# Moving and resizing the convolution chunks of four batches in a fused conv and low-rank mixer kernel

## The chip, the cores and the metric

One NeuronCore of one Trainium2 chip runs the whole kernel. The metric is the device time of one execution in microseconds (us); each version was run several times and medians are quoted.

## The reference, cut to what matters

`x` is (8, 4224, 192) in float32. A causal depthwise convolution of seven taps with softmaxed weights, eight heads of 24 channels, gives `y`; then a low-rank mixer over the sequence and a channel MLP:

```python
out = np.einsum('hk,bskhg->bshg', w, x_unf)      # the conv: y
...
h = xt @ U @ V                                    # sequence mixing, rank 32
u = x + h.transpose(0, 2, 1)                      # here x is y
ch = np.maximum(u @ w_ch1, 0.0) @ w_ch2           # 192 -> 768 -> 192
return (u + ch).astype(np.float32)
```

## The kernel before: the parts that matter

Every batch has 33 tiles of 128 positions; eight tiles make one of 33 groups. The program is scheduled by hand. From batch 3 on it runs in stages: W1 of three groups (the wide matrix product, its relus on ScalarE and VectorE), then W2 of three groups in twelve pieces, with other work put between the pieces. A dictionary says what comes ahead of which piece: `c4:0:3:AAD` is the conv of batch 4, from head 0, three heads, whose results are copied out of PSUM, the memory that matmuls write (evacuated), in turn by ScalarE (A), ScalarE and VectorE (D); `t` is the projection by U, `s` its sum, `h` the product with V, `x5:3` starts the shift copies of batch 5.

```python
        elif k < 10:
            b = k - 2
            at = {
                1: [f"c{b}:0:3:AAD"],
                2: [f"c{b}:3:3:AAD"],
                3: [f"c{b}:6:2:A"] + ([f"x{b + 1}:3"] if b + 1 < B else []),
                5: [f"t{b}", hs[0]],
                7: [f"s{b}"],
                8: [hs[1]],
                11: [hs[2]],
            }
```

The conv of a head is eight matmuls into two PSUM banks (there are eight, taken in rotation). Half of them read `xb`, a copy of x in which half of the partitions are shifted by a block:

```python
    def conv32(b, h0, nh, engs):
        ...
        for n in range(nh):
            ...
            pp = [bank(), bank()]
            for cg in range(4):
                t, w, st = (
                    (xt[b], bands[h // HQ][:, h % HQ, QB : 2 * QB], 1 + cg // 2)
                    if cg % 2
                    else (xbt[b], band2[:, h, :], cg // 2)
                )
                for r in range(2):
                    ...
                    nc.tensor.matmul(out=pp[r][...], lhsT=w[hr], rhs=t[hr, ...], ...)
            for part in range(2):
                evac(engs[(2 * n + part) % len(engs)], yt[b][...], pp[part][...])
```

GpSimd builds `xb` in six steps of a copy each (the second has a small copy more). There is one buffer for it, so the first copy for the next batch waits for the last conv matmul of this one. With `x5:3` three copies are issued right then; the others are issued one by one during the next W1, each behind a transfer of the x after that, and the transfers are held until W1 has come so far:

```python
        return [
            same(0, m),
            same(m, NB0, (NB0, NB1)),
            ahead(0, 0, m),
            ahead(0, m, NB0),
            ahead(1, 0, m),
            ahead(1, m, NB1),
        ]
...
        for g in gs1:
            ends = w1(g, RELU0 if g == 1 else RELU)
            for b, blocks in LOADS.items():
                for q, (gb, m) in enumerate(blocks):
                    if gb == g:
                        x_load(b, q, ends[m])
                        if steps:
                            steps.pop(0)()
```

Of the kernel before, what the change touches and what calls it, by code (L numbers as in the profile page):

```python
# [14 lines left out]
def kernel(  # L15
# [12 lines left out]
    B, S, D = x.shape  # L28
# [611 lines left out]
    for k in range(5, 14):  # L640
        gs = list(range(3 * k - 9, 3 * k - 6))
        hs = [f"h{g}" for g in range(nh, min(nh + 3, NG))] + [None] * 3
        nh = min(nh + 3, NG)
        if k == 5:
            at = {
                2: ["c3:0:3:AAD"],
                3: ["c3:3:3:AAD"],
                4: ["c3:6:2:A", "x4:3"],
                5: [hs[0]],
                6: ["t3"],  # L650
                8: ["s3", hs[1]],
                11: [hs[2]],
            }
        elif k < 10:
            b = k - 2
            at = {
                1: [f"c{b}:0:3:AAD"],
                2: [f"c{b}:3:3:AAD"],
                3: [f"c{b}:6:2:A"] + ([f"x{b + 1}:3"] if b + 1 < B else []),
                5: [f"t{b}", hs[0]],  # L660
                7: [f"s{b}"],
                8: [hs[1]],
                11: [hs[2]],
            }
        else:
            at = {0: [hs[0]], 4: [hs[1]], 8: [hs[2]]}
        SLOTS.append((gs, gs, {p: [w for w in what if w] for p, what in at.items()}))
# [180 lines left out]
```

## Time and profile before

| | kernel before |
|---|---|
| median of three runs | 325.3 us (325.18 to 325.31) |
| span of the profiled run | 323.5 us |
| TensorE busy | 317.1 us, 98% |
| ScalarE, VectorE, GpSimd busy | 170.4, 269.1, 142.7 us |
| stages of batches 3 to 7 | 28.30, 28.05, 28.28, 28.13, 28.12 us |

A stage is measured in the timeline, from the first matmul of its W1 to that of the next. In the chain of waits each line is start, duration and what the chain went through; in the timeline each line is start, duration, engine, source line, operation, tiles, shapes and count. L554 is W1, L583 W2, L339 the conv, L402 the projection, L305 the later shift copies, L568 ScalarE's relu. The lines themselves are in the prediction below.

### The profile page before, as it was taken

The numbers are of one execution on the slowest core, as the hardware profiler recorded it, in microseconds if no ns is written. First come the engines' busy times: TensorE is split into PE (matmuls) and PEld (weight loads), VectorE is DVE, ScalarE is ACT, GpSimd is POOL, SyncE is SP. The second block draws the span as 40 slices with busy tenths as digits, with TensorE's granted clock in tenths as the row PEclk, the third lists the DMA queues.
The fourth block names the chain that finished last, engine by engine and source line by source line (L and its number), as shares of the span: only waits on it lengthen the run. The fifth ranks groups of instructions, "written<-read, shape, count | busy, mean of one in ns | idle before, by whom it ended". The sixth has DMA issues, their size and how long they took to land.

```text
span 323.5 us, 9584 instructions
## 1 busy us (share of the span) xinstructions
PE 317.1 (98%) x3996; PEld 223.2 (69%) x3996; DVE 269.1 (83%) x551; ACT 170.4 (53%) x344; POOL 142.7 (44%) x111
## 2 busy tenths in 40 slices
PE   6999999999999999999999999999999999999996
PEld 3757676478677647866864784587797497487495
DVE  6769989987977986998798699879898897896864
ACT  1766624860874397088339708824903902912920
POOL 8664179729947694786859497000000000000000
PEclk9999999999999999999999999999999999999999
DMA  8999993999996899699699976139269059048035
GB/s 104 192 192 178 209 211 99 203 195 248 210 153 180 229 175 169 170 162 195 166 238 183 192 162 181 33 112 244 58 168 267 8 149 268 25 121 271 2 119 176
DMA packets 122907, 53.52 MB, mean 165 GB/s; under 512 B 87760, under 2 KB 122832, under 8 KB 122864
## 3 DMA queue, kind: packets, MB, share of 16 engines
q1 hardware_dynamic: 84528, 38.08, 47.0%
q0 software_dynamic: 38192, 14.73, 39.6%
q8 instruction: 31, 0.51, 0.7%
q14 instruction: 12, 0.10, 0.1%
q10 hardware_dynamic: 144, 0.10, 0.1%
HBM read 29.49 MB, written 25.95 MB: 171 GB/s over the span
## 4 chain that ended last, share of the span: by engine, by line
PE 92%; ACT 3%; DMA 2%; DVE 1%; issue 0%; POOL 0%; POOLq 0%
PE ps L583 42%; PE ps L554 39%; PE ps L339 3%; PE ps L457 3%; DMA x_sb<-in_x_dram 2%; PE ps L402 2%; ACT rl_sb L568 2%; PE ps L369 1%; ACT y_sb L256 1%; PE ps L509 1%; DVE u_sb L479 1%; DVE rl_sb L570 1%; PE ps L524 0%; PE ps L428 0%; POOL x_sb L79 0%
## 5 line engine op out<-in xcount | busy, mean ns | idle before, releaser
L568 ACT ACTIVATE rl_sb<-ps 128x512 bf16<-128x512 f32 x233 | 124.3, 603 | 108.0 <-PE ps L554 96.0
L583 PE MATMUL ps<-W_sb,rl_sb 128*128 128x192 bf16 x1584 | 141.9, 246 | 0.2
L583 PEld LDWEIGHTS <-rl_sb 128*128 128x128 bf16 x1584 | 128.1, 98 | 13.5 <-issue 13.1
L554 PE MATMUL ps<-uT,W_sb 64*128 64x512 bf16 x1188 | 131.7, 376 | 0.0
L570 DVE TENSOR_SCALAR rl_sb<-ps 128x512 bf16<-128x512 f32 x163 | 105.3, 688 | 15.7 <-PE ps L554 15.4
L554 PEld LDWEIGHTS <-W_sb 64*128 64x128 bf16 x1188 | 66.9, 94 | 60.5 <-issue 3.9
L592 DVE TENSOR_TENSOR out_sb<-ps,u_sb 128x384 f32<-128x384 f32 (+1 forms) x133 | 70.4, 550 | 25.9 <-PE ps L583 25.4
L305 POOL COPY xb_sb<-x_sb 32x3072 bf16<-32x3072 bf16 (+1 forms) x24 | 67.6, 2826 | 0.7
L479 DVE TENSOR_TENSOR u_sb<-y_sb,ps 128x192 bf16<-128x192 bf16 (+1 forms) x168 | 66.3, 461 | 0.0
L293 POOL COPY xb_sb<-x_sb 128x3072 bf16<-128x3072 bf16 x12 | 32.6, 2744 | 34.6 <-PE ps L339 25.7
L256 ACT ACTIVATE y_sb<-ps 128x384 bf16<-128x384 f32 (+4 forms) x90 | 38.2, 514 | 10.7 <-PE ps L339 7.9
L79 POOL DMA_DIRECT2D x_sb<-in_x_dram x32 | 27.1, 849 | 17.5 <-PE ps L554 10.5
L258 DVE CAST y_sb<-ps 128x408 bf16<-128x408 f32 (+4 forms) x36 | 19.2, 578 | 1.1 <-PE ps L369 0.9
L457 PE MATMUL ps<-tt_sb,V_sb 32*128 32x192 bf16 x264 | 12.4, 246 | 0.1
L339 PE MATMUL ps<-xb_sb,band 64*32 64x384 bf16 x192 | 12.1, 332 | 0.0
L339 PE MATMUL ps<-x_sb,band 64*32 64x384 bf16 x192 | 12.1, 333 | 0.0
L457 PEld LDWEIGHTS <-V_sb 32*128 32x128 bf16 x264 | 4.7, 92 | 7.3 <-issue 7.3
L416 ACT ACTIVATE tt_hi<-ps 128x192 bf16<-128x192 f32 x8 | 2.6, 331 | 10.9 <-PE ps L402 10.9
L369 PE MATMUL ps<-x_sb,band 64*64 64x240 bf16 (+3 forms) x192 | 8.1, 276 | 0.3 <-DMA x_sb<-in_x_dram 0.3
L369 PEld LDWEIGHTS <-band 64*64 64x64 bf16 x192 | 6.0, 106 | 2.2 <-issue 1.5
L339 PEld LDWEIGHTS <-band 64*32 64x32 bf16 x384 | 4.5, 89 | 4.1 <-issue 3.0
L402 PE MATMUL ps<-y_sb,U_sb 128*32 128x192 bf16 x258 | 7.4, 247 | 0.0
(65 smaller groups left out, 69.0 us busy)
## 6 DMA issues: line engine op xcount, KB each, us to landing
out_dram<-out_sb SPq DMA_DIRECT2D x131, 192.0 KB, 2.7
x_sb<-in_x_dram POOLq DMA_DIRECT2D x14, 384.0 KB, 7.3
x_sb<-in_x_dram POOLq DMA_DIRECT2D x7, 432.0 KB, 7.3
x_sb<-in_x_dram POOLq DMA_DIRECT2D x7, 408.0 KB, 8.0
x_sb<-in_x_dram POOLq DMA_DIRECT2D x1, 504.0 KB, 7.6
uT<-u_sb SPq DMA_TRANSPOSE x31, 3.9
x_sb<-in_x_dram POOLq DMA_DIRECT2D x1, 480.0 KB, 5.9
W_sb<-in_moe_w_ch_dram POOLq DMA_DIRECT2D x2, 192.0 KB, 7.6
```

Of the source, the lines that this page charges most:

```text
L79: return nc.gpsimd.dma_start(out=xt[b][HB * r : HB * r + HB, s0:s1, :], in_=x[b, blk * HB : (blk + s1 - s0) * HB, :].rearrange("(j p) d -> ...
L256: nc.scalar.activation(out=out, in_=in_, func=ACT.Copy)
L293: nc.gpsimd.tensor_copy(out=xbt[b][:, s0:s1, :], in_=xt[b][:, s0 + 1 : s1 + 1, :])
L305: nc.gpsimd.tensor_copy(out=xbt[b][q, s0:s1, :], in_=xt[b][q, s0:s1, :])
L339: nc.tensor.matmul(out=pp[r][QB * cg : QB * cg + QB, 0 : nk[r] * GS], lhsT=w[hr], rhs=t[hr, st : st + 2 * nk[r] - 1 : 2, hs], start=True, ...
L457: nc.tensor.matmul(out=banks[pr][:, a * D : (a + 1) * D], lhsT=V_sb[32 * q : 32 * q + 32, (j // 8) * 2 + j % 2, :], rhs=ttb[b][32 * q : 32 ...
L479: nc.vector.tensor_tensor(out=u_group(g)[:, i : i + n, :, hf, :], in0=yt[b][:, run[0] : run[0] + n, :].rearrange("p n (c k) -> p n c k", c=3),
L554: last = nc.tensor.matmul(out=pps[m][hf][:], lhsT=W1_sb[HB * hf : HB * hf + HB, c, m * P : (m + 1) * P], rhs=uTt[g][HB * hf : HB * hf + HB ...
L568: nc.scalar.activation(out=rl[:, m, hf, :], in_=pp[hf][:], func=ACT.Relu)
L570: nc.vector.tensor_scalar_max(out=rl[:, m, hf, :], in0=pp[hf][:], scalar1=0.0)
L583: last = nc.tensor.matmul(out=cps[:, a * D : (a + 1) * D], lhsT=rlt[g][:, m, hf, (i + a) * P : (i + a + 1) * P], rhs=W2_sb[:, m, :], start ...
L592: nc.vector.tensor_tensor(out=o[:, 0:n, :].rearrange("p n (c k) -> p n c k", c=3), in0=cps[:, 0 : n * D].rearrange("p (n c k) -> p n c k", ...
```

## The change

The intent: let the conv of batches 4 to 7 begin right behind W1, in chunks of two, three and three heads in place of three, three and two, with the first chunk evacuated by ScalarE alone.

```diff
-                1: [f"c{b}:0:3:AAD"],
-                2: [f"c{b}:3:3:AAD"],
-                3: [f"c{b}:6:2:A"] + ([f"x{b + 1}:3"] if b + 1 < B else []),
+                0: [f"c{b}:0:2:A"],
+                2: [f"c{b}:2:3:AAD"],
+                3: [f"c{b}:5:3:AAD"] + ([f"x{b + 1}:3"] if b + 1 < B else []),
```

## The prediction

> **What bounds the kernel now.** I read the page first: parts 1, 2 and 4.
>
> ```profile
> PE 317.1 (98%) x3996; PEld 223.2 (69%) x3996; DVE 269.1 (83%) x551; ACT 170.4 (53%) x344; POOL 142.7 (44%) x111
> ...
> PEclk9999999999999999999999999999999999999999
> ...
> PE 92%; ACT 3%; DMA 2%; DVE 1%; issue 0%; POOL 0%; POOLq 0%
> ```
>
> TensorE is busy for 98% of the span at full clock, and 92% of the chain that ended last is TensorE's own work. ScalarE, which the change fills better, has half its span free. So the change can matter only where it alters TensorE's sequence or makes it wait.
>
> Next, the chain of waits in order of time, for the stage that holds the convolution (conv) of batch 5 (137.58 to 165.86 us; batches 4, 6 and 7 have the same shape in the stages from 109.54, 165.86 and 193.99):
>
> ```profile
> 137.58 11.92 PE ps L554 x108
> 149.50 1.10 PE ps L583 x12
> 150.60 0.64 PE ps L339 x19
> 151.24 1.09 PE ps L583 x12
> 152.33 0.71 PE ps L339 x17
> 153.04 1.10 PE ps L583 x12
> 154.14 0.47 PE ps L339 x11
> 154.61 2.09 PE ps L583 x24
> 156.70 0.85 PE ps L402 x33
> ```
>
> L554 is W1 of three groups, L583 pieces of W2, L339 the three conv blocks (3, 3 and 2 heads), L402 the projection by U that needs all of y. All of it is TensorE, and every microsecond added or saved here is one of the kernel.
>
> Last, the timeline, for what finishes near the end of W1: the stage of batch 4 on TensorE and GpSimd, and that of batch 6.
>
> ```profile
> 121.23 1.16 PE L583 MATMUL ps<-W_sb,rl_sb 128*128 128x192 bf16 x12
> ...
> 118.58 3.08 POOL L305 COPY xb_sb<-x_sb 32x3456 bf16<-32x3456 bf16 x1
> 121.59 0.88 POOL L79 DMA_DIRECT2D x_sb<-in_x_dram  x1
> ...
> 177.56 1.16 PE L583 MATMUL ps<-W_sb,rl_sb 128*128 128x192 bf16 x12
> ...
> 174.90 3.08 POOL L305 COPY xb_sb<-x_sb 32x3456 bf16<-32x3456 bf16 x1
> ```
>
> W2 starts right behind W1 at 121.23. The last of the six GpSimd copies that build the shifted input xb of this very batch ends at 118.58 + 3.08 = 121.66, or 0.43 us later. The conv reads xb; today its first block stands behind one W2 piece and starts at 122.33, so the copy is hidden. In the stage of batch 5 the copy ends at 146.61 + 3.08 = 149.69 and W2 starts at 149.43; for batch 6 it is 177.98 against 177.56. For batch 7 the copies run through without transfers between them and end at 188.91 + 11.25 = 200.16, long before 205.68.
>
> **What the Trainium skill says.** "TensorE: Matmul & The Clock Gate", Step-by-step, says that only weight loads are pulled ahead and matmuls stay in program order. So if the first conv block waits, the W2 piece behind it waits too, although its data are ready. No wait in the trace of before contradicts it: block 2 of batch 5 held its last matmuls from 152.60 to 152.68 for a PSUM bank, and the W2 piece behind it came later by as much. "TensorEngine Tiling (Array Packing)", Key Properties, says that a change of tiling mode drains TensorE. The trace agrees: W2 matmuls start 0.0825 us apart, but from the last of a piece to the first of a conv block (150.351 to 150.527) it is 0.176, so 0.093 more. "Perfetto Trace Analysis", GPSIMD Engine Instruction, calls GpSimd spans unreliable and advises start-to-start spacing. Here the two nearly agree: 3.01 us from that copy to the next GpSimd instruction (118.58 to 121.59), 3.08 as its span. I take this 0.07 as the error of the copy's end. The same TensorE page, Part 1, has a clock that falls after about 3.4 us of idleness; the waits below are under 0.5 us, and the granted clock of all stages is 1.00, so I charge nothing.
>
> **The change part by part.** Number of matmuls, weight loads, evacuations, bytes: the same. Evacuations of a batch were AADAAD + AADAAD + AAAA, 12 by ScalarE and 4 by VectorE; they become AAAA + AADAAD + AADAAD, again 12 and 4. Only the order on TensorE moves: W1, piece, 3 heads, piece, 3 heads, piece, 2 heads, two pieces becomes W1, 2 heads, two pieces, 3 heads, piece, 3 heads, two pieces.
>
> *Saved.* The four stretches of W2 (12, 12, 12 and 24 matmuls) become three (24, 12, 24). Start to start they take 1.094, 1.093, 1.10 and 2.08 us; the new ones 2.08, 1.10 and 2.08. That is 5.37 against 5.26: one drain less, 0.10 us per batch, 0.4 us over four. I assume that going from W1 to conv costs what going from W1 to W2 does (about 0.1 us: last W1 pair at 177.243, W2 at 177.556, less 0.216 for the pair).
>
> *Added.* The conv now stands where W2 stood, so it must wait for the last xb copy. For the latency from an engine's end to TensorE I use the one such wait beside it: ScalarE's fourth evacuation ended at 152.630 and the matmul that wanted its bank started at 152.681, so 0.05. Waits: batch 4, 121.66 + 0.05 - 121.23 = 0.48; batch 5, 149.69 + 0.05 - 149.43 = 0.31; batch 6, 177.98 + 0.05 - 177.56 = 0.47; batch 7, none. Sum 1.26 us.
>
> The copies' end cannot drift to hide this: the GpSimd chain in a stage (four issues of the next x with copies between) is set off by the first matmuls of W1 and ends 12.1 us after the stage's start in all three stages (121.66 - 109.54, 149.69 - 137.58, 177.98 - 165.86), while W1 takes 11.76 (11.92 for batch 5, whose slow W1 is why its wait is smaller). The conv's end, which frees xb for the next copies, comes some 0.2 us later than before; the copies then wait 2.3 to 3.2 us for the next W1 anyhow, so nothing follows from it.
>
> *Unmoved.* PSUM banks rotate by eight. The first block takes four banks of W1's third and fourth row-blocks, evacuated by 149.01 at the latest for batch 5, before 149.43: no wait. The block at the second place finds its banks free, since the first block's four ScalarE evacuations (about 0.39 us apart and 0.51 for the last, from 0.42 after the block's start) are done about 2.1 us after it started, and the block starts 0.47 + 2.08 = 2.55 after. The last block inherits the 0.08 us bank wait of today's second block, for the same spacing of 0.64 + 1.10. The projection needs the last evacuation: by the same durations ScalarE is done about 2.1 us after the last block began, and the projection comes 0.71 + 2.08 = 2.79 after: free, as today.
>
> *Sum.* 1.26 - 0.41 = +0.85 us: per stage +0.38, +0.21, +0.37 and -0.10. 325.3 + 0.85 = 326.1 us.
>
> **The rivals.** First, the intended gain: ScalarE, idle 0.96 us ahead of its first conv evacuation today, is filled, one drain goes, and no wait comes. For it: the drain is real and ScalarE's backlog from W1 is the only engine queue in sight. Against it: the copy ends after W1 in three of the four stages. It would give 325.3 - 0.4 = 324.9 us; reality lies here if xb's dependence is met earlier than the recorded end of the copy. Second, the first block waits for ScalarE: W1's last relu ends at 149.99 for batch 5, 0.56 us after the block's place. If the block's banks were the last ones of W1, each batch would lose about 0.6, less 0.1 for the drain, so about +2.0 us, 327.3 us. The bank count above speaks against it. Even if some bank is late, this wait and the copy's run side by side and don't add. Third, the last block, now of three heads and nearer the projection in work, makes the projection wait for its evacuations: the slack of 0.7 us above says no; if ScalarE's queue were half a microsecond longer it would still cost nothing, and a wait of 0.3 us in four batches would make it 327.3.
>
> **Range and chances.** The copy's end is uncertain by 0.07 us in three stages (0.2 us), the drain by half (0.2 us), W1's hiccup of 0.16 us comes and goes, and the runs of before spread by 0.13. The first rival's side is bounded by 324.9, the second's and third's by 327.3. I take 325.3 to 326.8 us for 8 times in 10. Two per cent is 6.5 us. All conv blocks of the four batches together are 4 x 1.82 = 7.3 us, so nothing saves that; to lose it, each batch would have to wait 1.6 us, more than three times the longest wait found. Faster 0.005, within 2% 0.98, slower 0.015.
>
> **What would show it.** In the changed kernel's chain: L339 directly behind L554 with a hole of some 0.3 to 0.5 us (a wait on xb from GpSimd) for batches 4, 5 and 6 and none for batch 7; stage lengths of about 28.4, 28.5, 28.5 and 28.0 us against 28.04, 28.28, 28.13 and 28.12; one L583 stretch of 2.08 us right behind the first block; the last block with 0.71. Wrong would be: no hole (then 324.9), a hole that ends with a ScalarE relu, a hole for batch 7 too, or a projection that waits for y.

## The result, and the profile after

| | before | changed |
|---|---|---|
| median (six runs each) | 325.21 us | 326.36 us |
| fastest, slowest | 325.11, 325.31 | 326.19, 326.64 |
| stages of batches 4 to 7 | 28.05, 28.28, 28.13, 28.12 | 28.42, 28.48, 28.50, 28.02 |

The ratio is 1.0036 (95% interval 1.0023 to 1.0049): clearly slower, and well within 2%.

The page of the changed kernel, its first line and its chain by engine:

```profile
span 324.9 us, 9583 instructions
...
PE 85%; POOL 7%; ACT 3%; DMA 2%; DVE 1%; issue 1%; POOLq 0%
```

GpSimd, which had 0% of the chain before, now has 7%. The share is not the loss: the chain follows the copies back through W1, under which they run. The loss is what TensorE waits, and it is in the timeline at the end of batch 4's W1, on TensorE and on GpSimd:

```profile
121.56 0.33 PE L339 MATMUL ps<-xb_sb,band 64*32 64x384 bf16 x1
122.04 0.33 PE L339 MATMUL ps<-xb_sb,band 64*32 64x408 bf16 x1 [0.15 <-POOL xb_sb L305]
...
118.91 3.08 POOL L305 COPY xb_sb<-x_sb 32x3456 bf16<-32x3456 bf16 x1
```

The first conv matmul, which reads the half of xb already copied, starts at 121.56; the second needs the other half and starts at 122.04, 0.05 after the copy's end (118.91 + 3.08 = 121.99). The profile calls only 0.15 us of it idle, because the first matmul's modelled end covers the rest: read the wait from start to start, 0.48 us. The chain of waits of that stage, and the first lines of batch 7's, show the same:

```profile
118.91 3.10 POOL xb_sb L305
122.00 0.04 issue
122.04 0.54 PE ps L339 x10
122.58 2.09 PE ps L583 x24
124.67 0.64 PE ps L339 x19
125.31 1.09 PE ps L583 x12
126.40 0.71 PE ps L339 x17
127.11 2.09 PE ps L583 x24
129.20 0.85 PE ps L402 x33
...
195.28 11.76 PE ps L554 x108
207.04 0.47 PE ps L339 x11
207.51 2.09 PE ps L583 x24
```

In batch 4's stage the copy stands between W1 and the conv. In batch 7's, where no transfers of a next x come between the copies, the conv follows W1 directly. ScalarE's last relu of W1 ends at 122.28 in batch 4's stage, 0.23 us after the block has gone on, so it cannot be what held the block. The W2 pieces are now 24, 12, 24 and the last conv block shows the 0.71 that the middle one had.

### The profile page after: what moved, and what is told of

It reads as the page before. It is cut to its first block, busy times and chain, and to the rows that moved or that the text cites. A ratio compares the mean times of both kernels' runs of the same rounds, so it can differ in the third digit from the quotient of the medians.

```text
span 324.9 us, 9583 instructions
## 1 busy us (share of the span) xinstructions
PE 318.1 (98%) x3996; PEld 224.0 (69%) x3996; DVE 268.7 (83%) x551; ACT 170.3 (52%) x344; POOL 142.9 (44%) x111
## 4 chain that ended last, share of the span: by engine, by line
PE 85%; POOL 7%; ACT 3%; DMA 2%; DVE 1%; issue 1%; POOLq 0%
PE ps L583 41%; PE ps L554 32%; POOL xb_sb L305 5%; PE ps L339 3%; PE ps L457 3%; DMA x_sb<-in_x_dram 2%; PE ps L402 2%; ACT rl_sb L568 2%; POOL x_sb L79 2%; PE ps L369 1%; ACT y_sb L256 1%; PE ps L509 1%; DVE u_sb L479 1%; DVE rl_sb L570 1%; PE ps L524 0%
## 5 line engine op out<-in xcount | busy, mean ns | idle before, releaser
L339 PE MATMUL ps<-xb_sb,band 64*32 64x384 bf16 x192 | 13.1, 332 | 0.3 <-POOL xb_sb L305 0.3
```

The costliest lines, as they stand in the source:

```text
L339: nc.tensor.matmul(out=pp[r][QB * cg : QB * cg + QB, 0 : nk[r] * GS], lhsT=w[hr], rhs=t[hr, st : st + 2 * nk[r] - 1 : 2, hs], start=True, ...
```

## The experiments

The theory at this point: the added time is the wait of the first block for the last xb copy in the stages of batches 4, 5 and 6, less one TensorE drain in every stage. The rivals: the block waits for ScalarE's relus of W1 or their PSUM banks; the last block of three heads makes trouble near the projection; or sizes and engines, not the place, matter.

**1. The changed kernel again** (no edit).

> The changed kernel once more, on the chip of the three runs beside it. All theories: 1.0 us (0.8 to 1.3) over before, stages of batches 4 to 7 of 28.42, 28.49, 28.50 and 28.02 us. It also asks whether the 0.33 us by which the first profile of the changed kernel was late before batch 4's stage belongs to the change: if it was chance of the start-up, the stage of batch 4 starts within 0.15 us of 109.54 in some profile of this kernel.

Measured: 326.47 us median (326.17 to 327.06), ratio 1.0031 (1.0015 to 1.0046); stages 28.41, 28.47, 28.49, 28.02. The stages repeat to 0.01 us. The profiled run again started batch 4's W1 late (109.90 against 109.47), so that part of the expectation was not met here; experiment 6, which differs only in who evacuates the first block, has the same stages from a start at 109.39, so the late start is most likely scatter, though no profile of the changed kernel itself shows an early one.

**2. The last copies earlier.** A fourth copy is issued in the stage before, in GpSimd's idle time.

```diff
-                4: ["c3:6:2:A", "x4:3"],
+                4: ["c3:6:2:A", "x4:4"],
...
-                3: [f"c{b}:5:3:AAD"] + ([f"x{b + 1}:3"] if b + 1 < B else []),
+                3: [f"c{b}:5:3:AAD"] + ([f"x{b + 1}:4"] if b + 1 < B else []),
```

> The changed kernel, with a fourth of the six xb copies issued in the stage before, in GpSimd's idle time, so that the last copy should end about 3 us before W1 does. Copy theory (the added time is the first block's wait for the last xb copy, less one drain per batch): the waits go, the stages take about 28.04 - 0.10 = 27.94, 28.1, 28.02 and 28.02 us, and the kernel about 0.4 us under before: 324.8. Bank theory (the first block waits for ScalarE's relus of W1): nothing changes, 326.2. Last-block theory (three heads so near the projection): nothing changes, 326.2.

Measured: 325.02 us median (324.92 to 325.04), ratio 0.9984 (0.9971 to 0.9996). The stages are 27.94, 28.17, 28.02, 28.02, that is 0.10 to 0.11 under before in all four. The chain of waits at batch 4 and GpSimd's timeline there:

```profile
109.51 11.76 PE ps L554 x108
121.27 0.47 PE ps L339 x11
121.74 2.09 PE ps L583 x24
...
115.41 3.08 POOL L305 COPY xb_sb<-x_sb 32x3456 bf16<-32x3456 bf16 x1
118.42 1.72 POOL L79 DMA_DIRECT2D x_sb<-in_x_dram  x2
```

The last copy ends at 118.49, 2.7 us before the conv starts, and the conv follows W1 as in batch 7. The bank and last-block rivals, which wanted no change, fall: with the copies out of the way nothing is left of the added stage time.

**3. The same early copy in the kernel before.** The two `:3` of before become `:4`, as above.

> The kernel before with the same earlier fourth copy, as a control: there the copy was hidden behind a W2 piece. Copy theory: no change, 325.2 plus or minus 0.1, stages of 28.04 to 28.28 as before. If the copies' order pays by itself ([...]earlier transfers of x), it is faster by the same 1.3 us as the changed kernel gains from it.

Measured: 325.24 us median (325.11 to 327.18), ratio 1.0001 (0.9981 to 1.0021); stages 28.04, 28.28, 28.13, 28.12. The early copy alone is worth nothing: before, a W2 piece hid the copy. (The profiled run was the longest, of 327.18; it had lost 1.9 us by the start of batch 4's W1.)

**4. The sizes without the move.**

```diff
-                1: [f"c{b}:0:3:AAD"],
-                2: [f"c{b}:3:3:AAD"],
-                3: [f"c{b}:6:2:A"] + ([f"x{b + 1}:3"] if b + 1 < B else []),
+                1: [f"c{b}:0:2:A"],
+                2: [f"c{b}:2:3:AAD"],
+                3: [f"c{b}:5:3:AAD"] + ([f"x{b + 1}:3"] if b + 1 < B else []),
```

> Chunks of two, three and three heads, but the first at the place where before had it, behind one W2 piece; so the sizes and the engines without the move. Copy theory: neither wait nor saved drain, each of the four stages within 0.05 us of before, 325.2. Last-block theory: this is as slow as the changed kernel, 326.2. Bank theory: 325.2, as W1's relus are done by then.

Measured: 325.54 us median (325.3 to 325.65), ratio 1.0000 (0.9987 to 1.0012); stages 28.06, 28.28, 28.13, 28.13. Sizes and engines are free of cost in the stages; the place is what counts. (The fastest run is some 0.2 us over before's; experiments 11 and 12 deal with that.)

**5. The move without the sizes.**

```diff
-                1: [f"c{b}:0:3:AAD"],
+                0: [f"c{b}:0:3:AAD"],
```

> The kernel before with its chunks of three, three and two, the first moved right behind W1; so the move without the new sizes. Copy theory: the same waits on the last xb copy as in the changed kernel, and one drain less. Beyond that, by the bank count, the bank wait of 0.08 us that any three-head block shows one W2 piece behind another goes, as the second block now comes two pieces behind the first and the third has two heads only. Stages about 28.34, 28.41, 28.42 and 27.94 us; the kernel about 0.5 us over before, or 0.3 to 0.5 under the changed one. If the sizes of two, three and three are needed for the first block to fit behind W1 (a first block of three heads waits for W1's last banks), the stages are longer than those of the changed kernel, batch 7's above 28.02.

Measured: 326.07 us median (325.86 to 326.37), ratio 1.0020 (1.0005 to 1.0036); stages 28.34, 28.40, 28.42, 28.06. Where the copy sets the pace (batches 4, 5, 6) the stages are as expected, 0.08 under the changed kernel's. Batch 7 came 0.12 over its 27.94: a first block of three heads does meet W1's banks. Experiment 8 shows whose.

**6. The first block by ScalarE and VectorE in turn.**

```diff
-                0: [f"c{b}:0:2:A"],
+                0: [f"c{b}:0:2:AD"],
```

> The changed kernel with the first block evacuated by ScalarE and VectorE in turn in place of ScalarE alone. Copy theory: nothing on TensorE's path, the four stages within 0.05 us of 28.42, 28.49, 28.50 and 28.02, 326.3. If leaving VectorE out of the first block is what keeps its W2 evacuations in time, the two W2 pieces behind the block wait for banks and the stages grow by 0.1 us or more.

Measured: 326.08 us median (326.01 to 329.37, four runs), ratio 1.0054 (1.0014 to 1.0094, widened by the one run of 329.37); stages 28.41, 28.47, 28.49, 28.02. Which engine evacuates the first block does not matter to TensorE here.

**7. A longer copy.** One more small copy, of the same values, behind the last one.

```diff
-            ahead(1, m, NB1),
+            ahead(1, m, NB1, (NB0, NB1) if b > 3 else None),
...
+                if again:
+                    t = slice(*again)
+                    nc.gpsimd.tensor_copy(out=xbt[b][q, t, :], in_=xt[b][q, t, :])
```

> The changed kernel with one more small copy (two blocks of 32 partitions, written again with the same values) behind the last xb copy of batches 4 to 7, some 0.5 us of GpSimd, as such a copy takes in the trace of before. Copy theory: each wait of batches 4, 5 and 6 grows by just that, stages about 28.95, 29.0 and 29.0, batch 7's stays at 28.02, the kernel 1.5 to 1.6 us over the changed one, 327.8. If TensorE waited for something that merely ends at about the same time (relus, banks), nothing changes.

Measured: 328.12 us median (328.0 to 328.27), ratio 1.0083 (1.0068 to 1.0098); stages 28.98, 29.04, 29.06, 28.02. The chain of waits at batch 4 (line numbers are shifted by three):

```profile
118.56 3.09 POOL xb_sb L305
121.65 0.05 issue
121.70 0.52 POOL xb_sb L308
122.25 0.54 PE ps L342 x10
```

The copy adds 0.52 plus 0.05 between the two, and the three stages grow by 0.56 each; batch 7's doesn't. So in these three stages it is this copy that TensorE waits for.

**8. A version meant to beat both.** Early copy, chunks of three, three and two, first behind W1, for batch 3 too.

```diff
-                2: ["c3:0:3:AAD"],
-                3: ["c3:3:3:AAD"],
-                4: ["c3:6:2:A", "x4:3"],
+                0: ["c3:0:3:AAD"],
+                2: ["c3:3:3:AAD"],
+                3: ["c3:6:2:A", "x4:4"],
...
-                1: [f"c{b}:0:3:AAD"],
+                0: [f"c{b}:0:3:AAD"],
...
-                3: [f"c{b}:6:2:A"] + ([f"x{b + 1}:3"] if b + 1 < B else []),
+                3: [f"c{b}:6:2:A"] + ([f"x{b + 1}:4"] if b + 1 < B else []),
```

> A version meant to beat both: the fourth xb copy early, chunks of three, three and two with the first right behind W1, for batch 3 as well (its copies end 2.4 us before W1 does). Copy theory: per batch one drain (0.10) and one bank wait (0.08) less, no wait on xb; stages of batches 3 to 7 about 28.12, 27.87, 28.10, 27.95 and 27.94 against 28.30, 28.05, 28.28, 28.13 and 28.12; the kernel 0.9 us under before, 324.3. If the first block of three heads meets W1's banks, 0.3 us less of that gain per batch, so slower than the early copy alone.

Measured: 325.12 us median (324.9 to 325.49), ratio 0.9992 (0.9979 to 1.0005), no gain clear of noise; stages of batches 3 to 7 28.17, 27.98, 28.10, 28.06, 28.06. Only batch 5 met its figure; batches 4, 6 and 7 missed by 0.11 to 0.12, batch 3 by 0.05, and the kernel the 324.3 us expected. The chain of waits at batch 4:

```profile
109.45 9.86 PE ps L554 x90
119.31 2.55 ACT rl_sb L568 x5
121.86 0.04 issue
121.91 2.14 PE ps L583 x24
```

The three-head block takes six banks, so the W2 piece behind it takes the bank of W1's last ScalarE relu, which ends at 121.85; W2 starts 0.05 after it at 121.91, where block and drain alone would have allowed 121.14 + 0.64 = 121.78. With two heads first, W2's bank is one relu older. In batch 5 W1 itself is 0.16 us slower, and ScalarE has caught up. In batch 3 the relu ends at 93.69 and W2 starts at 93.74, 0.05 late, by the same wait. My bank count had stopped at the conv's own banks. This is what a first chunk of two is good for.

**9. Two heads first again, batch 3 too, and a bank freed sooner.** From experiment 2:

```diff
-                2: ["c3:0:3:AAD"],
-                3: ["c3:3:3:AAD"],
-                4: ["c3:6:2:A", "x4:4"],
+                0: ["c3:0:2:A"],
+                2: ["c3:2:3:AADADA"],
+                3: ["c3:5:3:AAD", "x4:4"],
...
-                2: [f"c{b}:2:3:AAD"],
+                2: [f"c{b}:2:3:AADADA"],
```

> The early copy with chunks of two, three and three again (a first block of three pushed the W2 piece behind it onto the bank of W1's last ScalarE relu and lost 0.12 us), also for batch 3, and the second block evacuated in the order AADADA, so that the bank that the third block's last matmuls want is VectorE's second and comes free some 0.4 us earlier. Bank theory of the 0.07 to 0.08 us: the third block takes 0.64 us from start to start in place of 0.71; stages of batches 3 to 7 about 28.12, 27.87, 28.10, 27.95 and 27.94 us; span 0.9 us under before, 324.3 in undisturbed runs. If that hold is not ScalarE's fourth evacuation, the block keeps 0.71 and the stages of batches 4 to 7 are those of the early copy: 27.94, 28.17, 28.02 and 28.02, 324.7.

Measured: 324.67 us median (324.48 to 324.85), ratio 0.9975 (0.9961 to 0.9988); stages 28.13, 27.87, 28.10, 27.95, 27.95, all as expected; the kernel was not (324.3, fastest run 324.48), which experiments 11 and 12 take up. The chain of waits at batch 4:

```profile
121.17 0.47 PE ps L339 x11
121.64 2.09 PE ps L583 x24
123.72 0.64 PE ps L339 x19
124.37 1.10 PE ps L583 x12
125.46 0.64 PE ps L339 x19
```

The last block takes 0.64 in place of 0.71: the hold was the bank that ScalarE emptied fourth.

**10. The early copy once more**, beside experiment 9.

> The early copy alone once more, beside the version above on one chip: 324.9 to 325.0 as in its first runs, stages of 27.94, 28.17, 28.02 and 28.02 us. A difference of the two versions under 0.3 us may drown in the start-up.

Measured: 325.15 us median (324.93 to 325.22), ratio 0.9989 (0.9976 to 1.0001); the four stages as in experiment 2; the fastest run, 324.93, lies in the 324.9 to 325.0 expected, the median 0.15 us above it. Of the two runs of this kernel, one interval lies just under 1 and one just includes it; by the stages it gains 0.43 us.

**11 and 12. One idle VectorE instruction.** The stages explain some 0.85 (0.86 in the first profile, 0.82 in the repeat) of the 1.08 us between the fastest runs of the two kernels. The other 0.2 is after them. From the first matmul of the last W1 to the last instruction, the kernel before takes 27.02 us, the changed one 27.21. All work there is the same; what differs is when VectorE performs its last wait for the program's end. The rows of that line for before and for the changed kernel (durations in ns as min, median and max; then first and last start in us):

```profile
L843 DVEq DRAIN  x2: 19/208/397, 320.3 to 323.0; - x2
```

```profile
L843 DVEq DRAIN  x2: 138/268/397, 321.5 to 324.5; - x2
```

The last one takes 19 ns and starts 0.50 us before the end of the first program, but takes 138 ns and starts 0.35 us before the end of the second, holding up the close. The changed program has one VectorE instruction fewer (705 against 706 in the trace; 9583 against 9584 in all), a semaphore wait that its order did not need. So I added an idle VectorE instruction to the changed kernel and to the version of experiment 9:

```diff
+    nc.vector.memset(rq[0:QB, 0:1], 0.0)
     wps = bank()
```

> The changed kernel plus one idle VectorE instruction at the start (a memset of a column that already holds the value). Of the 1.05 us between the fastest runs of the two kernels the four stages account for 0.84; in the traces so far the end of the program, from the last W1 to the last instruction, is 27.2 us in every kernel with 154 waits of VectorE's sequencer and 11 packets in the instruction queue q14, and 27.0 in those with 155 and 12. Length theory (the change shortened VectorE's program by one instruction, and so its last piece came later): back to 27.0 us at the end and 12 packets, stages unchanged at 28.42, 28.49, 28.50, 28.02, fastest runs 326.0 in place of 326.2. If the end is tied to the conv's order itself, 27.2 us and 326.2 stay.

Measured: 326.23 us median (325.99 to 328.44), ratio 1.0038 (1.0016 to 1.0060, again with a scattered run); fastest 325.99 as expected, end 27.00 us, stages unchanged at 28.41, 28.48, 28.50, 28.02. The medians and the ratio cannot resolve it; the fastest run and the trace can. The instruction queue had 13 packets, not the 12 expected: the thirteenth is a packet of 64 bytes at 0.14 us, which in the other traces falls before the span. What does go with the end in all fourteen traces is the last block of 8192-byte packets of that queue: in the six with an end of 27.0 us one starts 1.3 to 5.0 us before the end of the program, in the eight with 27.2 us none does, and the next starts 0.3 us after it. That fetching instructions is what delays the last wait was not tested.

> The best version so far plus the same idle VectorE instruction. Length theory: end of 27.0 us, stages of batches 3 to 7 as before (28.13, 27.87, 28.10, 27.95, 27.95), fastest run 324.3, median 0.9 us under before. Otherwise 324.5 as it was, and 0.7 us under.

Measured: 324.37 us median (324.2 to 324.52), ratio 0.9968 (0.9956 to 0.9980); end 27.02 us, stages 28.13, 27.87, 28.10, 27.95, 27.95. It is the best version.

All kernels in one table; the sum (of the rounded figures) is of the stages of batches 3 to 7, and the end is from the profiled run; "rest" is the fastest run less both:

| kernel | median | fastest | five stages | end | rest |
|---|---|---|---|---|---|
| before | 325.21 | 325.11 | 140.88 | 27.02 | 157.21 |
| changed | 326.36 | 326.19 | 141.72 | 27.21 | 157.26 |
| 2 early copy | 325.02 | 324.92 | 140.45 | 27.23 | 157.24 |
| 4 sizes only | 325.54 | 325.30 | 140.90 | 27.23 | 157.17 |
| 5 move only | 326.07 | 325.86 | 141.52 | 27.01 | 157.33 |
| 6 first by both | 326.08 | 326.01 | 141.69 | 27.02 | 157.30 |
| 7 longer copy | 328.12 | 328.00 | 143.40 | 27.23 | 157.37 |
| 8 three first, early | 325.12 | 324.90 | 140.37 | 27.23 | 157.30 |
| 9 two first, bank | 324.67 | 324.48 | 140.00 | 27.22 | 157.26 |
| 11 changed + 1 | 326.23 | 325.99 | 141.71 | 27.00 | 157.28 |
| 12 best + 1 | 324.37 | 324.20 | 140.00 | 27.02 | 157.18 |

Experiment 3 is left out, as its profiled run was a disturbed one; 1 and 10 repeat two of the kernels. The rest is the same to 0.2 us, while the stages differ by over 3 us: two numbers of one trace account to 0.2 us for the fastest runs of eleven kernels. The 0.2 us of the end is no larger than this scatter, so it rests on the traces and on experiments 11 and 12, not on this table.

## Why the prediction was right

- *The waits.* From the first to the second conv matmul: 0.48, 0.32 and 0.49 us in batches 4, 5 and 6, none in 7, against 0.48, 0.31, 0.47 and none. Experiments 2 (waits taken away) and 7 (waits made longer by a known 0.56) show the cause.
- *The drain saved.* 0.10 per stage, seen bare in batch 7 (28.12 to 28.02) and in all four stages of experiment 2. The assumption that W1 to conv costs what W1 to W2 does held: batch 7's W1 takes 11.76 us to the next matmul in both kernels.
- *The sum.* +0.85 us in the stages; measured +0.86 in the first profile and +0.82 in the repeat.
- *What the sum lacked.* The fastest runs lie 1.08 us apart, the medians 1.15. Of this 0.2 is the end of the program, which no step had looked for; experiments 11 and 12 show that one VectorE instruction more takes it away. Why a program one instruction shorter has its last VectorE wait late is not settled. What is left, up to 0.1, lies ahead of the stages and is put down to start-up scatter. So 326.36 lies in the range, 0.26 over the 326.1 of the sum, with a term in it that was not foreseen; that the range had room for it is luck.
- *The unmoved parts.* Right for the change as it was (the last block kept 0.71, the projection did not wait). The bank count was not complete, though: it did not ask for the bank of the W2 piece behind the first block. With two heads that bank is free; with three it is not, which cost 0.12 us in batch 7 of experiment 5 and in batches 4, 6 and 7 of experiment 8.
- *A slip without consequence.* The working has the conv end some 0.2 us later in its stage; by its own stage figures and in the traces it is 0.2 us in batch 5 alone and 0.4 in batches 4 and 6. The copies' end stayed where it was, 12.19 us after the first matmul of W1 in batch 4 of both kernels.
- *The hiccup of batch 5.* I let it come and go. It came in every trace (28.28 us or its like), so it belongs to the schedule; its cause stays open.
- *The rival of the full gain* had its mechanism right (one drain less, no wait), but only for batch 7, or with the copies early.

## What to carry to other kernels

When a block is moved forward on the busiest engine, list every input's end beside the new place, not only its banks and evacuations: a producer that was hidden by one piece of other work may now end too late (here by 0.3 to 0.5 us). If the producer has idle time, move it first; then the move pays. And count the buffers of the work that now follows the moved block as well as those of the block.

## What the Trainium skill lacked or had wrong

- "TensorEngine Tiling (Array Packing)", Key Properties, says that a change of tiling mode drains TensorE, but gives no price. Here it is 0.093 us from W2 to conv beyond the usual spacing, and one stretch less saves 0.10 to 0.11 us per stage. That this time is the drain is the page's word; the traces show its size.
- "Perfetto Trace Analysis", GPSIMD Engine Instruction, calls GpSimd spans unreliable. For these copies (3.08 us, 32x3456 bf16) the recorded end could be used: the matmul that waited started 0.05 us after it in all three stages, and the waits worked out from it were right to 0.02 us.
- The same page, in Matmuls, advises rotating PSUM banks so that evacuation overlaps; it doesn't say that the order of evacuating engines decides which bank comes back first. Here AADADA in place of AADAAD freed one sooner and took 0.07 us off a block.
- No page has the effect of a program's length on its end ("Runtime: NRT & Kernel Launch", Instruction fetch mechanics, has no time for it): 27.0 or 27.2 us for the same last work, changed by one idle VectorE instruction.
